# Sums of weight blocks by accumulating transfers, and signs moved into the forms: one core, retention and two dense layers

## The chip, the cores and the metric

The kernel runs on one core of one Trainium2 chip. The metric is device time in microseconds (us) of one execution; lower is better. The engines are TensorE (PE; its weight loads are listed as PEld), VectorE (DVE), ScalarE (ACT), GpSimd (POOL) and SyncE (SP), which only issues transfers here. Each engine works through its own instructions in order and waits on semaphores for the others.

## The reference

Three parts follow one another: retention (a recurrent state per head), a first dense layer with a hard-swish, and a second layer of eight experts whose results are weighted by a matrix P and summed.

```python
# retention: y[t] = scale * q[t] @ state;  state = gamma*state + k[t]^T v[t]
h = x @ w_in;  g = h * clip(h + 3, 0, 6) / 6;  x = g @ w_out     # 1536 x 512, 2048
logits = x @ w_gate
P = exp(logits - logits.max())                                   # 1536 x 8
# 8 times: P /= P.sum(1) + 1e-9;  P /= P.sum(0) + 1e-9;  P *= 1536 / 8
for e in range(8):
    h = maximum(x @ w1[e], 0)                                    # 512 -> 1024
    out += P[:, e:e+1] * (h @ w2[e])                             # 1024 -> 512
```

## The kernel before

All matmuls of the two layers take each float32 operand as a high part (rounded, by a ScalarE copy to the type fp32r) and a low part (what is left, by a VectorE subtraction), and sum three products: high x high, high x low, low x high. The helper `parts` makes the two parts.

The first layer goes through blocks of 512 tokens. `stage_a` makes h (12 matmuls), then ScalarE writes t (L353), VectorE multiplies it by h (L355), ScalarE writes its high part ghi (L358) and VectorE its low part glo (L360); `stage_b` multiplies by w_out two stages later. In the last block of the first layer (from step LASTB on) the loop also calls `next(forming)` four times a step: this prepares the second layer. In the same steps the gate's logits are made: `logits` multiplies on TensorE and copies to SBUF on ScalarE (tile l, L414), `logits_to_rows` transposes l on TensorE one step later (tile lt, L420).

The second layer works on two units of 768 tokens (unit u uses y2[u]). The weights of a unit go through 32 pairs of blocks (`pair(i)`, i from 0 to 63 over both units). The first expert matmul of a pair is a 2 x 2 block product done with seven products instead of eight (Winograd's variant of Strassen's method): the weights give seven forms (A11, A12, A22 and the sums S1 to S4 of blocks of 128 x 256), made by `w1_forms(i)` one pair ahead; the tokens give seven forms (B11, B21, B22 and the differences T1 to T4), made once per unit by `x_forms(u)` into tiles with one buffer each. `product` runs six matmuls of 384 columns for one product. `pair` combines the products in four PSUM banks: a copy to p, to u, to p again on ScalarE (L604), additions on VectorE (L603). A bank into which TensorE accumulates further has to be copied first: S3 x T3 goes into the bank that u was copied from. `relu_parts` splits the results (gh, gl); `outputs` multiplies them with w2 one iteration (two pairs) later, in chunks of three matmuls of 512 columns, spread between the products.

What sets the order: one Python program emits all instructions, and each engine takes its own in that order. Generators spread the small work: in the loop over pairs, after each product of a pair a `slot` passes, in which `outs` emits output chunks and `next(job)` is called twice (once in the first iteration), each call running `w1_forms` or `w2_parts` to its next `yield`. At the change of unit (pair 32), `forming` (the x forms of unit 1 and one set of weight forms) is started beside eight chunks of outputs that run alone. The loads: `load_pair(i, 0)` loads the two halves of w1 blocks for pair i, `load_pair(i, 1)` those of w2, all on SP, each into one of two buffers, two pairs ahead; SP waits until the buffer's old contents have been read.

## Time and profile before

| what | value |
|---|---|
| time, three runs | 1329.68, 1330.94, 1335.48 us; median 1330.94 us |
| span of the profiled execution (first to last instruction) | 1329.5 us; no separate time of this execution is given |
| TensorE busy | 1318.1 us, 99% of the span |
| VectorE busy | 897.7 us, 68% |
| ScalarE busy | 567.6 us, 43% |
| GpSimd busy | 26.7 us, 2% |
| DMA | 100.82 MB, mean 76 GB/s |

How to read it: an engine's busy time is the time in which it executed at least one instruction; an engine whose share is far below 100% can still be the one that others wait for at one place. The span runs from the first to the last instruction of one execution; the times are those of other executions without the profile.

### The profile page before, as it was taken

What the parts mean: (1) busy time and instruction counts of PE and PEld (TensorE: products, weight loads), DVE (VectorE), ACT (ScalarE), POOL (GpSimd) and SP (SyncE); (2) the same over time, 40 slices, a digit from 0 to 9 for tenths busy, and PEclk for the clock granted to TensorE, in tenths of its full rate; (3) what the DMA queues carried; (4) which work ended last, traced back from release to release, by engine and by line L of the source; (5) the groups of instructions that cost most, each with busy time, mean ns of one, the idle gap of its engine ahead of it and who ended that gap; (6) DMA issues with size and microseconds to landing.
All of it is one profiled execution on the core that took longest, in us unless ns stands there. A gap on an engine that the chain in (4) does not pass through costs nothing.

```text
span 1329.5 us, 17332 instructions
## 1 busy us (share of the span) xinstructions
PE 1318.1 (99%) x6776; PEld 1164.4 (88%) x6776; DVE 897.7 (68%) x1704; ACT 567.6 (43%) x1072; POOL 26.7 (2%) x30
## 2 busy tenths in 40 slices
PE   8999999999999999999999999999999999999998
PEld 7888888888888999999999998899999999999997
DVE  6877657338688666666666668766666666666663
ACT  5567445224534343434443344444343434443340
POOL 4300000000000000000000000000000000000000
PEclk9999999999999999999999999999999999999999
DMA  8633222002212122111221211312222111221201
GB/s 309 217 95 96 64 64 80 0 0 66 93 49 75 68 67 76 64 64 64 67 77 65 78 64 57 119 64 76 68 67 77 64 64 64 71 73 65 79 17 48
DMA packets 44990, 100.82 MB, mean 76 GB/s; under 512 B 3430, under 2 KB 3430, under 8 KB 44908
## 3 DMA queue, kind: packets, MB, share of 16 engines
q1 hardware_dynamic: 44908, 99.71, 22.2%
q8 instruction: 53, 0.87, 0.3%
q14 instruction: 29, 0.24, 0.1%
HBM read 96.55 MB, written 3.15 MB: 75 GB/s over the span
## 4 chain that ended last, share of the span: by engine, by line
PE 90%; DVE 3%; ACT 1%; DMA 0%; issue 0%; ACTq 0%
PE acc L660 38%; PE h L585 33%; PE acc L375 10%; PE h L348 9%; DMA raw<-in_we 0%; DVE gl L596 0%; DVE xl L501 0%; DVE w1lo L501 0%; DVE o L673 0%; DVE w2lo L501 0%; PE l L405 0%; DVE o L669 0%; DVE p L603 0%; ACT w2hi L500 0%; ACT xh L500 0%
## 5 line engine op out<-in xcount | busy, mean ns | idle before, releaser
L585 PE MATMUL h<-xh,w1hi 128*128 128x384 f32 x896 | 301.8, 337 | 0.9 <-ACT p L604 0.9
L660 PE MATMUL acc<-w2hi,gl 128*128 128x512 f32 x768 | 301.7, 393 | 0.0
L585 PE MATMUL h<-xh,w1lo 128*128 128x384 f32 x896 | 301.1, 336 | 0.0
L585 PE MATMUL h<-xl,w1hi 128*128 128x384 f32 x896 | 300.8, 336 | 0.2 <-DVE xl L501 0.2
L660 PE MATMUL acc<-w2hi,gh 128*128 128x512 f32 x768 | 299.6, 390 | 0.0
L660 PE MATMUL acc<-w2lo,gh 128*128 128x512 f32 x768 | 298.8, 389 | 0.0
L673 DVE SCALAR_TENSOR_TENSOR o<-acc,pm,o 128x512 f32<-128x512 f32 x174 | 130.7, 751 | 143.7 <-PE acc L660 143.7
L585 PEld LDWEIGHTS h<-xl,w1hi 128*128 128x128 f32 x896 | 168.2, 188 | 20.3 <-DVE xl L501 0.9
L585 PEld LDWEIGHTS h<-xh,w1hi 128*128 128x128 f32 x896 | 168.3, 188 | 19.8 <-ACT p L604 1.6
L660 PEld LDWEIGHTS acc<-w2hi,gl 128*128 128x128 f32 x768 | 144.1, 188 | 30.9
L585 PEld LDWEIGHTS h<-xh,w1lo 128*128 128x128 f32 x896 | 168.2, 188 | 0.0
L660 PEld LDWEIGHTS acc<-w2lo,gh 128*128 128x128 f32 x768 | 144.3, 188 | 13.0
L660 PEld LDWEIGHTS acc<-w2hi,gh 128*128 128x128 f32 x768 | 143.8, 187 | 13.0
L604 ACT ACTIVATE p<-h 128x384 f32<-128x384 f32 x128 | 62.9, 491 | 203.2 <-PE h L585 203.1
L501 DVE TENSOR_TENSOR w1lo<-raw,w1hi 128x512 fp32r<-128x512 f32 (+1 forms) x128 | 71.1, 555 | 77.4 <-ACT w1hi L500 77.3
L501 DVE TENSOR_TENSOR w1lo<-s,w1hi 128x512 fp32r<-128x512 f32 x128 | 87.9, 688 | 37.9 <-ACT w1hi L500 37.7
L604 ACT ACTIVATE u<-h 128x384 f32<-128x384 f32 x64 | 31.5, 492 | 173.5 <-PE h L585 173.5
L595 ACT ACTIVATE gh<-p 128x384 fp32r<-128x384 f32 x128 | 66.7, 521 | 57.5 <-DVE p L603 57.5
L501 DVE TENSOR_TENSOR w2lo<-raw,w2hi 128x512 fp32r<-128x512 f32 x128 | 87.2, 683 | 4.7 <-ACT w2hi L500 4.7
L595 ACT ACTIVATE gh<-u 128x384 fp32r<-128x384 f32 x64 | 33.6, 525 | 127.3 <-DVE u L603 127.3
L500 ACT ACTIVATE w1hi<-s 128x512 fp32r<-128x512 f32 x128 | 79.7, 624 | 3.3 <-DVE s L520 1.9
L348 PE MATMUL h<-xhi,wlo 128*128 128x512 f32 x192 | 74.9, 390 | 0.5 <-DVE wlo L136 0.5
(107 smaller groups left out, 1681.3 us busy)
## 6 DMA issues: line engine op xcount, KB each, us to landing
raw<-in_we SPq DMA_DIRECT2D x128, 512.0 KB, 3.4
raw<-in_wf SPq DMA_DIRECT2D x32, 512.0 KB, 3.7
qk<-in_qk SPq DMA_DIRECT2D x12, 512.0 KB, 6.9
kv<-in_kv SPq DMA_DIRECT2D x12, 512.0 KB, 6.0
out<-o SPq DMA_DIRECT2D x12, 256.0 KB, 2.0
tab<-in_tab SPq DMA_DIRECT2D x1, 40.5 KB
gk<-in_gk SPq DMA_DIRECT2D x1, 24.0 KB, 3.5
wg_raw<-in_wg SPq DMA_DIRECT2D x1, 16.0 KB, 7.7
```

The source lines that it names most:

```text
L348: nc.tensor.matmul(h, w[:, ks], x[:, k], start=(n == 0), stop=(n == 3 * KT - 1))
L375: nc.tensor.matmul(acc_b[i], l, r, start=(f == 0 and j == 0), stop=(f == nf - 1 and j == 2))
L500: nc.scalar.activation(out=hi, in_=t, func=AF.Copy)
L501: nc.vector.tensor_tensor(out=lo, in0=t, in1=f32(hi), op=ALU.subtract)
L585: nc.tensor.matmul(bank[:, 0:SB], l[:, w, ks], r[:, k], start=(start and n == 0), stop=(stop and n == 5), skip_group_check=True,)
L595: nc.scalar.activation(out=hi, in_=t, func=AF.Relu)
L604: copy = lambda out, a: nc.scalar.activation(out=out, in_=a, func=AF.Copy)
L660: nc.tensor.matmul(acc, l[:, cs], r[:, f % 2], start=(f == 0 and k == 0), stop=(f == 3 and k == 2))
L673: nc.vector.scalar_tensor_tensor(out=o[:, tt], in0=acc, scalar=sc, in1=o[:, tt], op0=ALU.mult, op1=ALU.add)
```

## The change

The four sums S1 to S4 of a pair's weight blocks are no longer formed by VectorE from the raw tile. `load_sums` builds them while loading: one plain transfer on SP writes block a21 four times (a broadcast read) into the tile s, then three transfers on POOL with the accumulate operation add further blocks from the weights in memory: a22 to the first three parts, a11 to the last three of four, as `block(1, 1, 3)` and `block(0, 0, 3)`, and a12 to the third. The sums are therefore all-plus sums, and the order of the forms changes to S1, S2, S4, S3. The raw tile holds only a11, a12 and a22 (two loads on SP). The signs that this takes away move to other places: `parts` can make the negative of a form (scale -1 in the ScalarE copy, another VectorE operation for the low part), used for B11 and B22; two copies in `pair` carry the scale -1; one addition becomes a subtraction. `x_forms` makes T1, T2, T4 and T3 in one buffer, xt, that is rewritten in place. `w1_forms` has three steps instead of seven, `x_forms` seven instead of nine, and `load_pair(i + 2, 0)` stands at the end of `w1_forms(i)`.

```diff
--- before.py
+++ after.py
@@ -482,23 +482,49 @@
 
 
 
-    A11, A12, A22, S1, S3, S2, S4 = range(7)
+    A11, A12, A22, S1, S2, S4, S3 = range(7)
     B11, T2, T1, T3, B21, B22, T4 = range(7)
-    xf, w1_t, w2_t, raw1, raw2, q_t = {}, {}, {}, {}, {}, {}
+    xf, w1_t, w2_t, raw1, raw2, q_t, sum_t = {}, {}, {}, {}, {}, {}, {}
 
     def load_pair(i, part):
         if i >= NIT:
             return
         f = 2 * (i % NPR)
-        t = pools["m2" if part else "m"].tile([P, 2, BLK], F32, tag=f"raw{part}", name=f"raw{part}", bufs=2)
-        nc.sync.dma_start(
-            out=t, in_=we_in[f:f + 2, :, part * BLK:(part + 1) * BLK].rearrange("t p c -> p t c")
-        )
-        (raw1, raw2)[part][i] = t
-
-    def parts(hi, lo, t):
-        nc.scalar.activation(out=hi, in_=t, func=AF.Copy)
-        nc.vector.tensor_tensor(out=lo, in0=t, in1=f32(hi), op=ALU.subtract)
+        if part == 0:
+            t = pools["m"].tile([P, 3, BLK // 2], F32, tag="raw0", name="raw0", bufs=2)
+            nc.sync.dma_start(out=t[:, 0:2], in_=we_in[f, :, 0:BLK].rearrange("p (k c) -> p k c", k=2))
+            nc.sync.dma_start(out=t[:, 2], in_=we_in[f + 1, :, BLK // 2:BLK])
+            raw1[i] = t
+            load_sums(i)
+            return
+        t = pools["m2"].tile([P, 2, BLK], F32, tag="raw1", name="raw1", bufs=2)
+        nc.sync.dma_start(out=t, in_=we_in[f:f + 2, :, BLK:2 * BLK].rearrange("t p c -> p t c"))
+        raw2[i] = t
+
+    def load_sums(i):
+
+        f = 2 * (i % NPR)
+        H2 = BLK // 2
+        t = pools["m"].tile([P, 4, H2], F32, tag="s", name="s", bufs=2)
+
+        def block(r, k, n):
+            a = we_in[f + r, :, k * H2:(k + 1) * H2].rearrange("p (o c) -> p o c", o=1)
+            return a.to_broadcast([P, n, H2]) if n > 1 else a
+
+        nc.sync.dma_start(out=t, in_=block(1, 0, 4))
+        nc.gpsimd.dma_start(out=t[:, 0:3], in_=block(1, 1, 3), accum_op=ALU.add)
+        nc.gpsimd.dma_start(out=t[:, 1:4], in_=block(0, 0, 3), accum_op=ALU.add)
+        nc.gpsimd.dma_start(out=t[:, 2:3], in_=block(0, 1, 1), accum_op=ALU.add)
+        sum_t[i] = t
+
+    def parts(hi, lo, t, sign=1):
+        nc.scalar.activation(out=hi, in_=t, func=AF.Copy, scale=float(sign))
+        if sign > 0:
+            nc.vector.tensor_tensor(out=lo, in0=t, in1=f32(hi), op=ALU.subtract)
+        else:
+            nc.vector.scalar_tensor_tensor(
+                out=lo, in0=t, scalar=-1.0, in1=f32(hi), op0=ALU.mult, op1=ALU.subtract
+            )
 
     def w1_forms(i):
 
@@ -506,23 +532,13 @@
         H2 = BLK // 2
         hi = pools["m"].tile([P, 7, H2], F32R, tag="w1hi", name="w1hi", bufs=2)
         lo = pools["m"].tile([P, 7, H2], F32R, tag="w1lo", name="w1lo", bufs=2)
-        a11, a12, a21, a22 = (r[:, f, k * H2:(k + 1) * H2] for f in range(2) for k in range(2))
-        t = pools["m"].tile([P, 4, H2], F32, tag="s", name="s", bufs=2)
-        parts(hi[:, A11:A12 + 1], lo[:, A11:A12 + 1], r[:, 0].rearrange("p (k c) -> p k c", k=2))
-        yield True
-        nc.vector.tensor_tensor(out=t[:, S1 - S1], in0=a21, in1=a22, op=ALU.add)
-        yield True
-        nc.vector.tensor_tensor(out=t[:, S3 - S1], in0=a11, in1=a21, op=ALU.subtract)
-        yield True
-        nc.vector.tensor_tensor(out=t[:, S2 - S1], in0=t[:, S1 - S1], in1=a11, op=ALU.subtract)
-        parts(hi[:, A22], lo[:, A22], a22)
-        yield True
-        nc.vector.tensor_tensor(out=t[:, S4 - S1], in0=a12, in1=t[:, S2 - S1], op=ALU.subtract)
-        load_pair(i + 2, 0)
+        t = sum_t.pop(i)
+        parts(hi[:, A11:A22 + 1], lo[:, A11:A22 + 1], r)
         yield True
         for n in range(2):
-            parts(hi[:, S1 + 2 * n:S3 + 1 + 2 * n], lo[:, S1 + 2 * n:S3 + 1 + 2 * n], t[:, 2 * n:2 * n + 2])
+            parts(hi[:, S1 + 2 * n:S1 + 2 * n + 2], lo[:, S1 + 2 * n:S1 + 2 * n + 2], t[:, 2 * n:2 * n + 2])
             yield True
+        load_pair(i + 2, 0)
         w1_t[i] = (hi, lo)
 
     def w2_parts(i):
@@ -542,37 +558,32 @@
         )
         xf.clear()
 
-        def form(n, t):
+        def form(n, t, sign=1):
             xf[n] = tuple(pools["xf"].tile([P, 2, SB], F32R, tag=f"x{n}{p}", name=f"x{p}") for p in "hl")
-            parts(*xf[n], t)
-
-        def tmp():
-            t = pools["m"].tile([P, 4, BLK // 2], F32, tag="s", name="s", bufs=2)
-            return t.rearrange("p a b -> p (a b)")[:, 0:2 * SB].rearrange("p (k c) -> p k c", k=2)
-
-        form(B11, b11)
+            parts(*xf[n], t, sign)
+
+        t = pools["m"].tile([P, 2, SB], F32, tag="xt", name="xt", bufs=1)
+
+        def into(a, b):
+            nc.vector.tensor_tensor(out=t, in0=a, in1=b, op=ALU.subtract)
+
+        form(B11, b11, -1)
         yield True
         form(B21, b21)
         yield True
-        t1 = tmp()
-        nc.vector.tensor_tensor(out=t1, in0=b12, in1=b11, op=ALU.subtract)
-        t2 = tmp()
-        nc.vector.tensor_tensor(out=t2, in0=b22, in1=t1, op=ALU.subtract)
+        into(b12, b11)
+        form(T1, t)
         yield True
-        form(T2, t2)
+        into(b22, t)
+        form(T2, t)
         yield True
-        form(T1, t1)
+        into(b21, t)
+        form(T4, t)
         yield True
-        t4 = tmp()
-        nc.vector.tensor_tensor(out=t4, in0=b21, in1=t2, op=ALU.subtract)
-        t3 = tmp()
-        nc.vector.tensor_tensor(out=t3, in0=b22, in1=b12, op=ALU.subtract)
+        into(b12, b22)
+        form(T3, t)
         yield True
-        form(T3, t3)
-        yield True
-        form(B22, b22)
-        yield True
-        form(T4, t4)
+        form(B22, b22, -1)
         yield True
 
     def product(i, bank, w, x, start, stop):
@@ -601,12 +612,12 @@
         tmp = lambda n: pools["m2"].tile([P, SB], F32, tag=n, name=n, bufs=2)
         bank = lambda n: ps_s.tile([P, BLK], F32, tag=n, name="h")
         add = lambda out, a, b: nc.vector.tensor_tensor(out=out, in0=a, in1=b, op=ALU.add)
-        copy = lambda out, a: nc.scalar.activation(out=out, in_=a, func=AF.Copy)
+        copy = lambda out, a, sign=1: nc.scalar.activation(out=out, in_=a, func=AF.Copy, scale=float(sign))
 
         bx = bank("s0")
         product(i, bx, A11, B11, True, True)
         p1 = tmp("p1")
-        copy(p1, bx[:, 0:SB])
+        copy(p1, bx[:, 0:SB], -1)
         yield
         by = bank("s1")
         product(i, by, A12, B21, True, True)
@@ -614,7 +625,7 @@
         add(p1, by[:, 0:SB], p1)
         product(i, bx, S2, T2, False, True)
         u2 = tmp("u2")
-        copy(u2, bx[:, 0:SB])
+        copy(u2, bx[:, 0:SB], -1)
         yield
         relu_parts(i, 0, 0, p1)
         bz = bank("r")
@@ -628,7 +639,7 @@
         product(i, bz, S4, B22, False, True)
         relu_parts(i, 1, 1, p5)
         yield
-        add(u2, bz[:, 0:SB], u2)
+        nc.vector.tensor_tensor(out=u2, in0=u2, in1=bz[:, 0:SB], op=ALU.subtract)
         product(i, bx, A22, T4, False, True)
         yield
         relu_parts(i, 0, 1, u2)
```

What this moves, on ScalarE, at three places. First the last block of the first layer, from the second stage that ScalarE handles beside the forms on (xh are the x forms' high parts, w1hi those of the weight forms, l the copy of the logits). Before:

```order
L353 ACTIVATE t<-h,three 128x512
L358 ACTIVATE ghi<-t 128x512
L500 ACTIVATE xh<-s 128x768 x2
L353 ACTIVATE t<-h,three 128x512
L358 ACTIVATE ghi<-t 128x512
L500 ACTIVATE xh<-s 128x768
L500 ACTIVATE xh<-x_726 128x768
L500 ACTIVATE xh<-s 128x768
L500 ACTIVATE w1hi<-raw_2480 128x512
L414 ACTIVATE l<-l 128x384
L353 ACTIVATE t<-h,three 128x512
L358 ACTIVATE ghi<-t 128x512
```

With the change (L521 is the copy in `parts`, L500 before):

```order
L353 ACTIVATE t<-h,three 128x512
L358 ACTIVATE ghi<-t 128x512
L521 ACTIVATE xh<-xt 128x768 x4
L353 ACTIVATE t<-h,three 128x512
L358 ACTIVATE ghi<-t 128x512
L521 ACTIVATE xh<-x_726 128x768
L521 ACTIVATE w1hi<-raw_2480 128x768
L521 ACTIVATE w1hi<-s 128x512 x2
L414 ACTIVATE l<-l 128x384
L353 ACTIVATE t<-h,three 128x512
L358 ACTIVATE ghi<-t 128x512
```

The four difference forms stand together ahead of the next t, and three copies of weight forms, two of them from s, stand between ghi and the second l; before, there was one between them.

Second, the change of unit (pair 32), from the first x forms of unit 1 on. Before:

```order
L500 ACTIVATE xh<-x_727 128x768 x2
L500 ACTIVATE xh<-s 128x768
L604 ACTIVATE p_7224<-h 128x384
L500 ACTIVATE xh<-s 128x768
L604 ACTIVATE u_7255<-h 128x384
L500 ACTIVATE xh<-s 128x768
L595 ACTIVATE gh<-p_7224 128x384
L604 ACTIVATE p_7275<-h 128x384
```

With the change (lines from `pair` on are 11 higher: L615 is the copy that was L604):

```order
L521 ACTIVATE xh<-x_727 128x768 x2
L521 ACTIVATE xh<-xt 128x768 x2
L615 ACTIVATE p_7203<-h 128x384
L521 ACTIVATE xh<-xt 128x768 x2
L615 ACTIVATE u_7236<-h 128x384
L521 ACTIVATE xh<-x_727 128x768
L606 ACTIVATE gh<-p_7203 128x384
L615 ACTIVATE p_7256<-h 128x384
```

The copy to u stands behind the high parts of all four difference forms; before, it stood behind those of two difference forms.

Third, the steady loop, one pair from its first copy to p on. Before:

```order
L604 ACTIVATE p_6767<-h 128x384
L500 ACTIVATE w1hi<-raw_6540 128x512
L500 ACTIVATE w1hi<-raw_6540 128x256
L604 ACTIVATE u_6803<-h 128x384
L500 ACTIVATE w1hi<-s 128x512
L595 ACTIVATE gh<-p_6767 128x384
L604 ACTIVATE p_6829<-h 128x384
L500 ACTIVATE w1hi<-s 128x512
L500 ACTIVATE w2hi<-raw_6582 128x512 x2
```

With the change:

```order
L615 ACTIVATE p_6610<-h 128x384
L521 ACTIVATE w1hi<-raw_6365 128x768
L521 ACTIVATE w1hi<-s 128x512 x2
L521 ACTIVATE w2hi<-raw_6396 128x512
L615 ACTIVATE u_6656<-h 128x384
L521 ACTIVATE w2hi<-raw_6396 128x512
L606 ACTIVATE gh<-p_6610 128x384
L615 ACTIVATE p_6681<-h 128x384
L606 ACTIVATE gh<-p_6681 128x384
```

All copies of the next pair's weight forms, and the first of w2, now stand ahead of the copy to u; before, two stood there.

## Rows read from the trace of the kernel before

**Rows 1.** The page, parts 1 and 2: busy time, and clock in 40 slices.

```profile
PE 1318.1 (99%) x6776; PEld 1164.4 (88%) x6776; DVE 897.7 (68%) x1704; ACT 567.6 (43%) x1072; POOL 26.7 (2%) x30
...
PEclk9999999999999999999999999999999999999999
```

**Rows 2.** Windows: stretch, length, busy us of each engine, clock, DMA share, GB/s.

```profile
325.00:345.00 20.00, 19.64 (x111) 17.72 (x110) 16.08 (x33) 12.17 (x26) 0.00 (x0) 1.00 0.38 127
375.00:800.00 425.00, 424.33 (x2134) 383.38 (x2133) 297.83 (x605) 169.78 (x352) 0.00 (x0) 1.00 0.20 67
800.00:830.00 30.00, 29.84 (x147) 26.15 (x146) 24.66 (x40) 14.66 (x27) 0.00 (x0) 1.00 0.17 62
830.00:860.00 30.00, 29.48 (x151) 26.67 (x150) 24.20 (x47) 14.37 (x30) 0.00 (x0) 1.00 0.38 132
860.00:1300.00 440.00, 440.00 (x2211) 398.28 (x2210) 295.53 (x564) 178.02 (x369) 0.00 (x0) 1.00 0.19 64
```

**Rows 3.** Timeline, ScalarE, two pairs: start, duration, instruction, idle before.

```profile
610.10 0.49 ACT L604 ACTIVATE p<-h 128x384 f32<-128x384 f32 x1 [2.66 <-PE h L585]
...
614.25 0.49 ACT L604 ACTIVATE u<-h 128x384 f32<-128x384 f32 x1 [2.83 <-PE h L585]
...
625.63 0.49 ACT L604 ACTIVATE p<-h 128x384 f32<-128x384 f32 x1 [2.66 <-PE h L585]
```

**Rows 4.** Groups by line and shape: busy us, mean ns.

```profile
L501 DVE TENSOR_TENSOR w1lo<-s,w1hi 128x512 fp32r<-128x512 f32 x128 | 87.9, 688 | 37.9 <-ACT w1hi L500 37.7
...
L500 ACT ACTIVATE w1hi<-s 128x512 fp32r<-128x512 f32 x128 | 79.7, 624 | 3.3 <-DVE s L520 1.9 <-DVE s L515 1.4
...
L513 DVE TENSOR_TENSOR s<-raw 128x256 f32<-128x256 f32 x64 | 26.8, 418 | 0.0
...
L159 DVE TENSOR_SCALAR w<-raw 128x512 uint32<-128x512 uint32 x32 | 14.5, 454 | 1.1 <-DMA raw<-in_wf 1.1
...
L501 DVE TENSOR_TENSOR xl<-s,xh 128x768 fp32r<-128x768 f32 x8 | 7.6, 956 | 2.3 <-ACT xh L500 2.3
...
L500 ACT ACTIVATE xh<-s 128x768 fp32r<-128x768 f32 x8 | 6.6, 837 | 8.3 <-DVE s L560 8.1 <-DVE s L569 0.3
```

**Rows 5.** The page, part 6: DMA issues, KB each, us to landing.

```profile
raw<-in_we SPq DMA_DIRECT2D x128, 512.0 KB, 3.4
...
qk<-in_qk SPq DMA_DIRECT2D x12, 512.0 KB, 6.9
...
out<-o SPq DMA_DIRECT2D x12, 256.0 KB, 2.0
```

**Rows 6.** Timeline, VectorE, last block of the first layer.

```profile
299.27 0.95 DVE L558 TENSOR_TENSOR s<-x 128x768 f32<-128x768 f32 x1
300.25 0.96 DVE L560 TENSOR_TENSOR s<-x,s 128x768 f32<-128x768 f32 x1
```

**Rows 7.** Timeline, ScalarE, the same stretch.

```profile
302.73 0.67 ACT L353 ACTIVATE t<-h,three 128x512 f32<-128x512 f32 x1
306.73 0.63 ACT L358 ACTIVATE ghi<-t 128x512 fp32r<-128x512 f32 x1 [3.33 <-DVE t L355]
...
310.00 0.47 ACT L414 ACTIVATE l<-l 128x384 f32<-128x384 f32 x1
```

**Rows 8.** The chain that ended last, the same stretch: start, us, what.

```profile
311.50 0.33 PE lt L420 x3
```

**Rows 9.** Timeline, VectorE, at the change of unit.

```profile
814.31 0.95 DVE L558 TENSOR_TENSOR s<-x 128x768 f32<-128x768 f32 x1
```

**Rows 10.** Timeline, ScalarE, at the change of unit.

```profile
817.47 0.49 ACT L604 ACTIVATE p<-h 128x384 f32<-128x384 f32 x1 [0.34 <-PE h L585]
...
820.94 0.49 ACT L604 ACTIVATE u<-h 128x384 f32<-128x384 f32 x1 [2.24 <-PE h L585]
```

**Rows 11.** Timeline, TensorE, the product S3 x T3 at the change of unit.

```profile
823.10 0.33 PE L585 MATMUL h<-xh,w1hi 128*128 128x384 f32 x1
823.60 0.45 PE L585 MATMUL h<-xl,w1hi 128*128 128x384 f32 x1 [0.16 <-DVE xl L501]
```

## The prediction

> **What bounds the kernel now.** Read the page first: TensorE is busy 1318.1 us of a span of 1329.5 us, and the granted clock is full in all forty slices [rows 1]. VectorE has 68% and ScalarE 43%. So the question is only where TensorE ever waits. The table by stage answers it for the second layer, which begins near 323 us: between 375 and 800 us TensorE idles 0.7 us of 425, between 860 and 1300 us not at all; 0.36 us are lost at the start of the layer and 0.7 us around the change of unit (800 to 860 us) [rows 2]. Work that is taken from VectorE or ScalarE in the steady loop can therefore return nothing. The loop's period is one pair of blocks: the copy of the first product begins at 610.10 us and one pair later at 625.63 us, so 15.53 us per pair [rows 3].
>
> **The change in the steady loop.** Removed from VectorE: four adds or subtracts of 128x256 per pair, 0.42 us each [rows 4], 1.7 us in all of a pair's 15.53; the two separate splits of the raw tile become one of 128x768. This is worth 0 us, since TensorE does not wait there [rows 2]. The other sign of a form and of an accumulation changes an instruction's scale or operation, not its size: 0 us.
>
> Moved: the splits of the next pair now stand together. On ScalarE the copy of the second result u used to follow one pass over the raw tile; now it follows a 128x768 copy (0.84 us, as the x form of that size), two of 128x512 (0.62 us each) and one w2 copy, taken at the same 0.62 us [rows 4]. From the end of the copy of p at 610.59 us that makes 613.3 us; TensorE does not release u before 614.25 us [rows 3]. So 0 us, with 0.95 us of cover. If the sums landed late, ScalarE would stand at its first copy from s, and u, p and the banks behind them would wait.
>
> Added: per pair one plain transfer of 512 KB on SP (instead of a part of the raw load) and three accumulating ones on POOL, 384, 384 and 128 KB. Each waits for the one before, and POOL takes them in order, so a pair costs POOL two waits for 384 KB and about one for 128 KB. With X and Y for the two sizes, the loop holds as long as 2X + Y stays under 15.53 us. No accumulating transfer is in the trace. A plain load of 512 KB lands in 3.4 us, a store of 256 KB in 2.0 us [rows 5]: 1.4 us per 256 KB and 0.6 us fixed. I count an accumulation as twice its bytes, because it reads the source and the old value: X = 0.6 + 3 x 1.4 = 4.8 us, Y = 2.0 us, 2X + Y = 11.6 us. The lower end counts the bytes once: 2.7 and 1.3, 6.7 us. The upper end takes the loads of the first stage, 6.9 us for 512 KB, and twice the bytes: 10.35 and 3.45, 24.2 us. I take 11.6 us, as DMA in this stage is busy only 0.19 to 0.20 at 64 to 67 GB/s [rows 2]; the change multiplies the bytes by 2304/1024, which with the extra reads of 896 KB makes about 0.6. It hides under TensorE's 15.53 us, with 3.9 us of cover: 0 us. The whole chain with its plain transfer takes 15.0 us, and with two buffers it has about two pairs, 31 us.
>
> The Trainium skill bears on this price. Its page "Collectives: The Full Stack" (section "The bandwidth ceiling: the fold count and why AG ≠ RS ≠ AR") says that an add inside a transfer costs two source reads, not cycles; its page "DMA: Bandwidth & Descriptors" (section "Anatomy of one DMA — SWDGE (gpsimd) path") gives 2.0 us plus bytes/436e3. By both, as an estimate, X would be 3.8 and Y 2.6, 2X + Y 10.2 us, and the sum the same.
>
> **The x forms, made twice, are where it costs.** Before, two temporaries of the tag s let VectorE run its subtractions back to back (299.27 and 300.25 us [rows 6]). Now one buffer xt is rewritten in place: subtract on VectorE, high part on ScalarE, low part on VectorE, and only then the next subtraction. A step takes 0.96 + 0.84 + 0.96 us [rows 4], 2.76 us, and there are four in a row.
>
> First place, the last block of the first layer. The chain starts at 299.27 us; its fourth high part ends at 299.27 + 3 x 2.76 + 0.98 + 0.84 = 309.4 us, and the order puts the activation t behind it, which ran at 302.73 us before [rows 7]. VectorE then does the fourth low part until 310.3 us, the reduction and t x h; ScalarE's second step ghi, 306.73 us before, starts at 311.2 us. Behind it come B22, the raw copy (768) and two copies from s, and only then l, the logits' copy: 311.2 + 0.54 + 0.74 + 0.75 + 1.05 = 314.25 us, ended 314.7 us, against a start of 310.00 us before. TensorE wants l for its transposes at 311.50 us [rows 8] and is in order, so the whole stream moves by 3.3 us. Nothing regains it: TensorE has no idle time behind. Bounds: 0 if l were not needed so soon, 5 if the steps run 10 to 15% slower.
>
> Second place, the change of unit. VectorE starts the first subtraction at 814.31 us [rows 9]; with 2.76 us per step and one accumulator update (0.66 us) between, the fourth high part ends at about 825.0 us. The copy of u, at 820.94 us before [rows 10], now stands behind it, ends near 825.5 us, and S3 x T3 needs its bank and the low part of T3, ready at 826.1 us. TensorE wanted that low part at 823.60 us [rows 11]. That is 2.5 us less about 0.3 us of the stalls that were there: +2.2 us, bounds 0 to 4.
>
> At the start of the second layer the load is less bunched but shares its DMA with the new transfers: 0 us, bounds -0.4 to +1.
>
> **Sum.** 3.3 + 2.2 = +5.5 us. On the profiled span of 1329.5 us that is 1335.0 us; the median of the three runs is 1.4 us above this span (1330.94), so I forecast 1336.4 us, +0.4%. About 0.5%, 6.65 us, is what a measurement of this kernel can tell from no change; so the forecast is "no change that can be told", near its edge.
>
> **Rivals.**
> A, slower by much: the accumulations are not hidden. If 2X + Y exceeds 15.53 us, POOL becomes the bound and every pair from the third on pays the excess, 62 times: X above 6.4 us decides it (Y at 0.4 X). At X = 7 the excess is 1.4 us and the time about 1423 us; at the upper end it is 8.6 us, 535 us more, about 1870 us. For it: 6.9 us for a plain 512 KB under load [rows 5]. Against it: 0.2 DMA share and 3.4 us in this very stage [rows 2, 5]. A mechanism of its own could bring it on: POOL kept from writing its descriptors while VectorE holds a common port. If each of the three waited for one of VectorE's longest instructions (0.96 us), 2X + Y would be 14.5 us, still hidden but with 1.0 us of cover. The Trainium skill's page "SBUF — State Buffer" ("The DVE blocks DMA trap (SWDGE)") states such a lock, for VectorE's faster two-port mode. The one-input operation of 128x512 takes 0.45 us, the two-input split w1lo<-s 0.69 us [rows 4], and the loop's splits are of the second kind.
>
> B, the x forms cost nothing: their stalls are covered in a way that I do not see, and the time is 1330 to 1332 us. For it: the page shows ScalarE idle more than half of the time [rows 1]. Against it: all engines work in order, and the places are fixed by the order.
>
> C, faster by over 0.5%: 6.65 us would have to come back, but the stages of the second layer hold 1.7 us of TensorE idle time altogether [rows 2]. Only a shorter spacing of matmuls could do it; nothing in the change touches that.
>
> **Chances.** Forecast (hidden transfers, two single stalls, 1332 to 1342 us) 0.64, of it 0.20 above 1337.6 us, since costs that I have not seen would add; B 0.08; A 0.25; C 0.03. So faster 0.03, same 0.44 + 0.08 = 0.52, slower 0.20 + 0.25 = 0.45. The range starts at 1330 us (C and half of B below it) and has to reach into A: up to 1400 us, an excess of 1.0 us per pair (X near 6.9 us), about half of A's weight; some 2 in 10 stay outside. The likeliest case's own range is 1332 to 1342 us.
>
> **What the profile after would show.** VectorE's busy time falls by some 110 us and TensorE's idle time does not fall. TensorE waits about 3 us for ScalarE's l before the second set of transposes near 311 us, and about 2 us near 823 us for u or the low part of T3. The accumulations on POOL land in 4 to 6 us, and no copy from s waits for DMA in the loop. The forecast is wrong if the period of a pair is above 15.53 us (A), if the two waits are missing (B), or if a third kind of wait appears, most likely in the first pairs, where a pair lasts only some 7 us and s, w1 and w2 loads come together.

## The result and the profile after

The changed kernel took 1347.31 us (median of 4 runs, 1346.28 to 1351.34); the kernel before, timed beside it, 1333.14 us (4 runs, 1329.68 to 1335.48). The ratio is 1.0114 [1.0094, 1.0134]: slower by 1.1%, some 14 us. That lies inside the range of 1330 to 1400 us, but the forecast of "no change that can be told" was missed: the median is 10.9 us above 1336.4 us. Six more runs of it (run 9) give 1.0099 [1.0076, 1.0122].

The page of the kernel after, parts 1 and 6 (KB each, us to landing), against [rows 1] and [rows 5]:

```profile
PE 1326.5 (99%) x6776; PEld 1170.4 (87%) x6776; DVE 812.7 (60%) x1384; ACT 565.4 (42%) x1008; POOL 248.1 (18%) x222
...
s<-in_we POOLq DMA_DIRECT2D x128, 384.0 KB, 5.0
s<-in_we SPq DMA_DIRECT2D x64, 512.0 KB, 5.4
...
s<-in_we POOLq DMA_DIRECT2D x64, 128.0 KB, 4.8
```

VectorE was relieved as intended, and TensorE, which bounds the kernel, is busy for 8.4 us longer with the same 6776 matmuls; 5.5 us of that lie ahead of the last block, which no edit touches (last section). An accumulation of 384 KB landed in 5.0 us (4.8 foreseen), the one of 128 KB in 4.8 us (2.0 foreseen).

The table by stage (busy us of each engine, clock, DMA share, GB/s), to be read beside [rows 2]:

```profile
375.00:800.00 425.00, 425.00 (x2142) 384.62 (x2142) 263.22 (x479) 171.85 (x332) 95.56 (x83) 1.00 0.70 154
...
830.00:860.00 30.00, 27.43 (x137) 24.05 (x136) 23.47 (x36) 16.38 (x30) 2.57 (x2) 1.00 0.62 160
860.00:880.00 20.00, 18.40 (x93) 16.39 (x93) 10.10 (x17) 7.12 (x14) 5.69 (x5) 1.00 0.71 152
880.00:1300.00 420.00, 420.00 (x2110) 380.38 (x2109) 249.07 (x409) 170.43 (x328) 92.29 (x80) 1.00 0.69 150
```

In the two long stretches TensorE never idles: in the loop the transfers are hidden. POOL's timeline there (start, duration, instruction, what ended the idle time before) shows one set of three in a pair, 15.43 us from one first transfer to the next:

```profile
599.81 1.28 POOL L515 DMA_DIRECT2D s<-in_we  x1 [5.22 <-DVE p L614]
604.83 1.28 POOL L516 DMA_DIRECT2D s<-in_we  x1 [3.74 <-DMA s<-in_we]
610.25 0.90 POOL L517 DMA_DIRECT2D s<-in_we  x1 [4.14 <-DMA s<-in_we]
615.24 1.28 POOL L515 DMA_DIRECT2D s<-in_we  x1 [4.10 <-DVE p L614]
```

What is lost is lost in single places. TensorE's waits (us in total, times, longest):

```profile
PE h L596 <- ACT u L615: 3.7, 2, 2.1
PE lt L420 <- ACT l L414: 3.5, 1, 3.5
PE h L596 <- ACT p L615: 1.9, 2, 1.6
```

The three that are not the wait for l, on TensorE's timeline (pair 1, the change of unit, and 30 us behind it):

```profile
344.44 0.45 PE L596 MATMUL h<-xh,w1hi 128*128 128x384 f32 x1 [1.63 <-ACT p L615]
...
837.16 0.44 PE L596 MATMUL h<-xh,w1hi 128*128 128x384 f32 x1 [2.07 <-ACT u L615]
...
866.95 0.44 PE L596 MATMUL h<-xh,w1hi 128*128 128x384 f32 x1 [1.60 <-ACT u L615]
```

Where the time went is read by landmarks on ScalarE that both programs have: the 42nd activation t of the first layer (the start of its last block, here), and the copies to u of pairs 0, 5, 31, 35 and 63. Lengths in us, worked out from ScalarE's timelines:

| profiled run | start | last block | first pairs (u0 to u5) | u5 to u31 | unit change (u31 to u35) | u35 to u63 |
|---|---|---|---|---|---|---|
| before | 279.21 | 46.71 | 69.46 | 405.27 | 63.60 | 434.93 |
| after | 283.45 | 53.12 | 71.13 | 404.70 | 68.40 | 433.89 |
| after, once more (run 9) | 278.26 | 51.75 | 72.33 | 404.70 | 69.09 | 433.95 |

Between before and after: +6.4 us in the last block, +1.7 in the first pairs, +4.8 at the unit change, -1.6 in the two stretches between, and +4.2 at the start, which no edit touches. Run 9 without the slow start: +5.0, +2.9, +5.5, -1.5 and -1.0, 10.9 us in all.

The -1.6 us are no gain in the loop. With the change ScalarE makes the copy to u later behind the copy to p in two of these pairs (4.44 us in pair 31 and 5.19 in pair 35, against 4.15 and 4.14 before), without TensorE waiting for it, so these landmarks move by themselves; and 1.1 us come back between pairs 5 and 6, ahead of the steady loop. The first copy to p of a pair does not: in each of these pairs ScalarE stands idle until TensorE releases it. By it:

| profiled run | last block (to p0) | first pairs (p0 to p6) | p6 to p31 | unit change (p31 to p35) | p36 to p63 |
|---|---|---|---|---|---|
| before | 44.63 | 84.33 | 388.33 | 63.61 | 419.40 |
| after | 51.04 | 85.14 | 388.33 | 67.65 | 419.40 |
| after, once more (run 9) | 49.67 | 86.36 | 388.33 | 68.38 | 419.40 |

So the steady loop is the same to the hundredth, and the loss is +6.4, +0.8 and +4.0 us in the profile after, +5.0, +2.0 and +4.8 us in run 9. The runs below give the u landmarks, and p where it matters.

**Last block.** ScalarE's timeline after, beside [rows 7]:

```profile
304.48 0.85 ACT L521 ACTIVATE xh<-xt 128x768 fp32r<-128x768 f32 x1 [1.63 <-DVE xt L568]
307.34 0.85 ACT L521 ACTIVATE xh<-xt 128x768 fp32r<-128x768 f32 x1 [2.02 <-DVE xt L568]
...
313.07 0.85 ACT L521 ACTIVATE xh<-xt 128x768 fp32r<-128x768 f32 x1 [2.02 <-DVE xt L568]
...
317.71 1.13 ACT L521 ACTIVATE w1hi<-s 128x512 fp32r<-128x512 f32 x2
318.75 0.47 ACT L414 ACTIVATE l<-l 128x384 f32<-128x384 f32 x1
```

The four high parts stand 2.86 us apart (2.76 foreseen), ScalarE idles about 2 us before each, and l comes at 318.75 us. With the later start of the block (4.24 us) taken off, that is 314.5 us, where 314.25 was foreseen. The windows over that place show more than a wait:

```profile
315.00:320.00 5.00, 1.45 (x8) 0.99 (x7) 4.26 (x7) 4.09 (x7) 0.00 (x0) 0.81 0.01 2
320.00:322.00 2.00, 2.00 (x6) 1.61 (x6) 1.30 (x3) 1.24 (x2) 0.00 (x0) 0.50 0.70 221
322.00:324.00 2.00, 2.00 (x6) 1.52 (x6) 1.96 (x4) 1.16 (x3) 0.00 (x0) 0.50 0.82 202
324.00:326.00 2.00, 2.00 (x9) 1.58 (x8) 0.53 (x3) 0.69 (x1) 0.01 (x1) 0.76 0.74 216
326.00:328.00 2.00, 2.00 (x10) 1.66 (x9) 1.30 (x2) 0.63 (x1) 1.26 (x1) 1.00 0.86 253
```

After the idle 3.5 us the granted clock is 0.50, the 1.2 GHz level, for about five microseconds: 6 matmuls per 2 us where 10 fit later. So a wait of 3.5 us costs 6.4 us.

**First pairs.** The wait of 1.63 us stands behind a w2 load that came late on ScalarE, not behind a sum:

```profile
340.18 0.63 ACT L521 ACTIVATE w2hi<-raw 128x512 fp32r<-128x512 f32 x1 [2.08 <-DMA raw<-in_we]
```

In run 9 it is the sums: there TensorE waits 0.93 us for p and 1.78 us for l, each behind a copy from s.

**Unit change.** SP issues the plain transfers of two sums at 843.35 and 848.84 us, because the sums before them were read only 5 us apart. POOL's timeline then:

```profile
847.91 1.28 POOL L515 DMA_DIRECT2D s<-in_we  x1 [18.84 <-DVE w1lo L523]
855.84 1.29 POOL L516 DMA_DIRECT2D s<-in_we  x1 [6.65 <-DMA s<-in_we]
861.77 0.91 POOL L517 DMA_DIRECT2D s<-in_we  x1 [4.64 <-DMA s<-in_we]
862.36 1.62 POOL L515 DMA_DIRECT2D s<-in_we  x1
868.11 1.28 POOL L516 DMA_DIRECT2D s<-in_we  x1 [4.12 <-DMA s<-in_we]
876.75 0.90 POOL L517 DMA_DIRECT2D s<-in_we  x1 [7.37 <-DMA s<-in_we]
```

and ScalarE's copies from these sums:

```profile
861.55 0.63 ACT L521 ACTIVATE w1hi<-s 128x512 fp32r<-128x512 f32 x1 [2.13 <-issue]
865.37 0.63 ACT L521 ACTIVATE w1hi<-s 128x512 fp32r<-128x512 f32 x1 [3.18 <-DMA s<-in_we]
...
879.75 0.63 ACT L521 ACTIVATE w1hi<-s 128x512 fp32r<-128x512 f32 x1 [2.39 <-DMA s<-in_we]
```

The first sum was whole 22 us after its plain issue, the second 31 us (to 879.75), for its three transfers had to stand behind the first one's on POOL. ScalarE, in order, holds u and p back until the sum is there. The first of these sums is TensorE's wait of 1.60 us at 866.95 us; at the second TensorE does not wait.

### The profile page after: what moved, and what is told of

Same layout as the page of the kernel before. It is cut to its first block, busy times and chain, and to the rows that moved or that the text cites. A ratio compares the mean times of both kernels' runs of the same rounds, so it can differ in the third digit from the quotient of the medians.

```text
span 1345.0 us, 17793 instructions
## 1 busy us (share of the span) xinstructions
PE 1326.5 (99%) x6776; PEld 1170.4 (87%) x6776; DVE 812.7 (60%) x1384; ACT 565.4 (42%) x1008; POOL 248.1 (18%) x222
## 4 chain that ended last, share of the span: by engine, by line
PE 88%; DVE 3%; ACT 1%; DMA 1%; issue 1%; POOL 0%; DVEq 0%; ACTq 0%; POOLq 0%
PE acc L671 38%; PE h L596 33%; PE acc L375 9%; PE h L348 9%; DMA s<-in_we 1%; DVE xl L523 1%; ACT xh L521 1%; DVE xt L568 1%; DMA raw<-in_we 1%; DVE w2lo L523 0%; DVE o L684 0%; DVE t L355 0%; DVE w1lo L523 0%; DVE x L392 0%; ACT w1hi L521 0%
## 5 line engine op out<-in xcount | busy, mean ns | idle before, releaser
L515 POOL DMA_DIRECT2D s<-in_we x64 | 87.5, 1366 | 425.5 <-DMA s<-in_we 312.5
L615 ACT ACTIVATE p<-h 128x384 f32<-128x384 f32 x128 | 62.8, 491 | 205.3 <-PE h L596 204.8
L516 POOL DMA_DIRECT2D s<-in_we x64 | 81.8, 1278 | 267.3 <-DMA s<-in_we 267.3
L614 DVE TENSOR_TENSOR p<-h,p 128x384 f32<-128x384 f32 x128 | 70.8, 553 | 95.0 <-PE h L596 95.0
L523 DVE TENSOR_TENSOR w1lo<-raw,w1hi 128x768 fp32r<-128x768 f32 x64 | 61.3, 957 | 90.2 <-ACT w1hi L521 90.2
L517 POOL DMA_DIRECT2D s<-in_we x64 | 57.6, 900 | 313.1 <-DMA s<-in_we 309.3
L523 DVE TENSOR_TENSOR w1lo<-s,w1hi 128x512 fp32r<-128x512 f32 x128 | 83.0, 685 | 11.7 <-ACT w1hi L521 11.7
```

The source lines that it names most:

```text
L515: nc.gpsimd.dma_start(out=t[:, 0:3], in_=block(1, 1, 3), accum_op=ALU.add)
L516: nc.gpsimd.dma_start(out=t[:, 1:4], in_=block(0, 0, 3), accum_op=ALU.add)
L517: nc.gpsimd.dma_start(out=t[:, 2:3], in_=block(0, 1, 1), accum_op=ALU.add)
L523: nc.vector.tensor_tensor(out=lo, in0=t, in1=f32(hi), op=ALU.subtract)
L614: add = lambda out, a, b: nc.vector.tensor_tensor(out=out, in0=a, in1=b, op=ALU.add)
L615: copy = lambda out, a, sign=1: nc.scalar.activation(out=out, in_=a, func=AF.Copy, scale=float(sign))
```

## The experiments

The theory: the loss has two causes, the chained x forms (a wait, and half clock behind it) and sums that come late where pairs are close together. Rivals: contention by 2304 KB a pair everywhere, one cause alone, or a loss no longer than the wait.

**Run 1, e1_xforms_as_before.** The changed kernel with the differences formed two at a time again.

```diff
-        def into(a, b):
+        def into(t, a, b):
...
-        into(b12, b11)
-        form(T1, t)
+        into(b11, b12, b11)
+        into(t, b22, b11)
         yield True
-        into(b22, t)
         form(T2, t)
         yield True
-        into(b21, t)
-        form(T4, t)
+        form(T1, b11)
...
```

> The changed kernel with the x forms made in the order of before: two differences ahead, then their parts (the second buffer is the x tile itself, written in place); the loads, the accumulating transfers and the signs stay. Theory (the in-place chain of the x forms is most of the loss: 3.5 us of waiting for the logits' copy, some 2.7 us of matmuls at half clock behind it, some 2 us at the change of unit): 8 us less than the changed kernel, so about 1339 us where the changed kernel has 1347; no wait for l near 315 us, granted clock 1.00 in that stretch. Rival (the accumulating transfers are the loss): within 2 us of the changed kernel.

Measured: 1343.84 us, ratio 1.0082 [1.0055, 1.0109]. The last block is 46.72 us, as before the change, and clock and wait of that place are gone. But the first pairs grew to 73.73 and the unit change to 70.99 us. ScalarE's timeline there:

```profile
855.47 0.63 ACT L521 ACTIVATE w1hi<-s 128x512 fp32r<-128x512 f32 x1 [6.40 <-issue]
858.83 0.63 ACT L521 ACTIVATE w1hi<-s 128x512 fp32r<-128x512 f32 x1 [2.73 <-DMA s<-in_we]
```

and TensorE's clock in the windows behind it:

```profile
860.00:862.00 2.00, 1.59 (x5) 1.59 (x6) 2.00 (x5) 1.59 (x4) 0.31 (x1) 0.50 0.81 167
862.00:864.00 2.00, 2.00 (x7) 1.71 (x6) 1.45 (x3) 0.71 (x2) 0.96 (x1) 0.50 0.76 199
```

The stalls of the x forms had given the sums time. Without them the wait for u behind the late sum grows from 1.6 to 5.4 us, with half clock behind it too, and in the first pairs TensorE waits 2.6 us for l. The two causes hide each other: undoing one returned 3.5 us by the medians, and by the profiles, from the last block on, only 0.2 us against after and 0.8 us against run 9.

**Run 2, e2_no_accumulation.** The three accumulating transfers left out.

```diff
         nc.sync.dma_start(out=t, in_=block(1, 0, 4))
-        nc.gpsimd.dma_start(out=t[:, 0:3], in_=block(1, 1, 3), accum_op=ALU.add)
-        nc.gpsimd.dma_start(out=t[:, 1:4], in_=block(0, 0, 3), accum_op=ALU.add)
-        nc.gpsimd.dma_start(out=t[:, 2:3], in_=block(0, 1, 1), accum_op=ALU.add)
```

> The changed kernel without the three accumulating transfers; it leaves out the additions to the sums, everything else runs. Theory (the x forms are most): only the waits of the first pairs of the second layer (some 2 us) and one after the change of unit (1.6 us) go, so 3 to 4 us less than the changed kernel, with the wait for l, the half clock and the wait at the change of unit as they are. Rival (the transfers are the loss): back to within 3 us of before.

Measured: 1340.33 us, ratio 1.0062 [1.0043, 1.0082]. First pairs 69.63 us (before: 69.46), unit change 66.90 (63.60), last block 53.29 (46.71). What stays is the x forms: 6.6 us in the last block and 3.3 us at the unit change, with TensorE's waits of 3.6 us for l and 2.1 us for u. The wait for u is as long as in the profile after, but here half clock follows it. Run 2:

```profile
833.00:835.00 2.00, 2.00 (x7) 1.91 (x7) 2.00 (x4) 0.83 (x2) 0.00 (x0) 0.50 0.37 133
```

and after, as far behind its own wait:

```profile
840.00:842.00 2.00, 1.75 (x9) 1.29 (x8) 2.00 (x4) 0.83 (x3) 0.00 (x0) 1.00 0.38 135
```

In runs 7 and 9 the same wait of 2.1 us brings 0.50 as well.

**Run 3, e3_both_undone.** Both edits above together.

```diff
-        nc.gpsimd.dma_start(out=t[:, 0:3], in_=block(1, 1, 3), accum_op=ALU.add)
...
-        into(b12, b11)
-        form(T1, t)
+        into(b11, b12, b11)
+        into(t, b22, b11)
...
```

> Both: x forms in the order of before, and no accumulating transfers (the additions to the sums are left out). Theory: the two parts are all there is, so within 2 us of before, although VectorE has some 110 us less to do; the relief of VectorE returns nothing. Rival (a further cost lies in the moved signs or in the splits that stand together in the loop): 3 us or more above before.

Measured: 1330.26 us, ratio 0.9982 [0.9964, 0.9999]; last block 46.70, first pairs 69.62, unit change 62.71 us. By p the first pairs take 83.54 us (84.33 before), the unit change 62.72 us (63.61) and the loops 388.33 and 419.40 us. The new signs and the new grouping of the splits cost nothing that shows; no third cause is left. From the last block on run 3 is 1.7 us shorter than before, in the stretches in which TensorE had idled before; that is all the relief of VectorE can have returned.

**Run 4, e4_late_logits_copy, and run 5, e5_short_logits_copy.** The kernel before with nothing but a later l: its second copy repeated 10 times, then 5 times.

```diff
-        nc.scalar.activation(out=l, in_=t[:, 0:SB], func=AF.Copy)
+        for _ in range(10 if n == 1 else 1):
+            nc.scalar.activation(out=l, in_=t[:, 0:SB], func=AF.Copy)
```

> The kernel before with one thing added: the second copy of the logits in the last block of the first layer is made ten times over (nine more of 0.49 us each, the same values), so that l comes late there and nowhere else. ScalarE issues such copies about 0.38 us apart, so l is 3.4 us later and TensorE waits some 2.5 to 3.4 us for it. Theory (a wait of this length also costs the clock behind it): some 5 to 6 us more than before, with a granted clock near 0.5 for 5 to 6 us after the wait. Rival (a wait costs only its length): 2.5 to 3.4 us more, clock 1.00.

> The kernel before with the second logits copy repeated 5 times instead of 10 (same output). Ten copies took 5.18 us and made TensorE wait 3.7 us, so 4 more copies of 0.52 us less the same slack of about 1.0 us give a wait of about 1.1 us. Theory (only the long pause brings the half clock behind it): the last-block segment grows by that wait alone, 46.7 to about 47.8 us, and the granted clock stays 1.00 from 310 to 330 us. Rival (the loss is in proportion to the wait, 6.7 for 3.7 us): about 48.7 us, with a stretch of lower clock behind the wait.

Measured: with ten copies 1338.04 us, ratio 1.0035 [1.0017, 1.0053], and the last block +6.7 us for a wait of 3.7 us; with five (one run, 1330.99 us) a wait of 1.1 us and the last block 48.02 us, +1.3. Windows with ten copies:

```profile
310.00:318.00 8.00, 4.27 (x13) 3.20 (x12) 2.95 (x7) 5.58 (x12) 0.00 (x0) 0.72 0.00 0
318.00:324.00 6.00, 6.00 (x23) 4.81 (x22) 3.00 (x8) 2.82 (x6) 0.00 (x0) 0.81 0.27 90
```

and with five:

```profile
310.00:318.00 8.00, 7.14 (x33) 5.99 (x34) 5.19 (x12) 5.02 (x10) 0.00 (x0) 1.00 0.19 61
318.00:324.00 6.00, 6.00 (x31) 5.26 (x30) 5.90 (x13) 2.22 (x5) 0.00 (x0) 1.00 0.28 99
```

The long wait lowers the clock, the short one does not, and the loss is not in proportion. A late l alone makes the last block's whole loss.

**Run 6, e6_one_more_accumulation.** One accumulating transfer of 384 KB twice.

```diff
         nc.gpsimd.dma_start(out=t[:, 1:4], in_=block(0, 0, 3), accum_op=ALU.add)
+        nc.gpsimd.dma_start(out=t[:, 1:4], in_=block(0, 0, 3), accum_op=ALU.add)
         nc.gpsimd.dma_start(out=t[:, 2:3], in_=block(0, 1, 1), accum_op=ALU.add)
```

> The changed kernel with the transfer that adds the first block a second time in three of the four sums (its sums are changed by that; the work of every engine but the queue is not). Theory (POOL's queue is full in the loop: the three transfers of a pair are issued 5.0, 5.4 and 5.0 us apart, 2X + Y = 11.6 us is its least by the prediction, and 15.53 us a pair is the limit): a fourth of 5.0 us makes about 16.6 us a pair, so the loop goes from 15.53 to about 16.6 us a pair, ScalarE waits for the sums in every pair, and the time is about 1347 + 60 x 1.07 = 1410 us. Rival (the transfers overlap, or the queue has room): the period stays 15.53 us and the time within 5 us of the changed kernel.

Measured: 1634.34 us (one run). The loop takes 530.98 / 26 = 20.4 us a pair, where the theory said 16.6 and its rival 15.53. POOL's timeline:

```profile
603.15 0.90 POOL L518 DMA_DIRECT2D s<-in_we  x1 [3.91 <-DMA s<-in_we]
603.74 1.61 POOL L515 DMA_DIRECT2D s<-in_we  x1
609.11 1.28 POOL L516 DMA_DIRECT2D s<-in_we  x1 [3.76 <-DMA s<-in_we]
619.09 1.28 POOL L517 DMA_DIRECT2D s<-in_we  x1 [8.70 <-DMA s<-in_we]
625.00 0.90 POOL L518 DMA_DIRECT2D s<-in_we  x1 [4.64 <-DMA s<-in_we]
```

POOL never waits for anything but its own transfers: it is the bound, as rival A had it. The size was missed because one of the transfers now lies beside the pair's loads on SP (512 KB for s at 607.56 us, 512 KB of w2 at 609.89 us), and it took 10.0 us where the others took 5.4 to 5.9; over the loop it took 6.3 to 10.0 us, 8.8 in the middle. In the changed kernel it is the small transfer that stands beside them, 4.8 us there and 3.0 us here. The clock falls too, to 0.91 from 600 to 700 us, since TensorE waits for u in nearly every pair (57 waits, 1.2 to 6.6 us, 194.5 us in all), but that lies under POOL's bound and adds nothing to it. The rows show one thing more: POOL issues the next sum's first transfer 0.59 us behind the small one (603.15, 603.74 us), so it does not wait for the small one to land.

**Run 7, e7_later_splits, and run 8, e8_xforms_and_later_splits.** In each pair the w2 splits go first, and the splits of the sums behind them, one a slot; run 8 has the x forms of run 1 as well.

```diff
-                    jobs.append([w1_forms(i + 1)] if ahead else [])
-                    jobs[-1].append(w2_parts(i))
+                    jobs.append([w2_parts(i)])
+                    jobs[-1] += [w1_forms(i + 1)] if ahead else []
...
-                        for _ in range(1 if not it or (alone and slot < 6) else 2):
+                        for _ in range(2 if alone and 6 <= slot <= 8 else 1):
```

> The changed kernel with the jobs of a pair in another order: the splits of the second-layer weights first, those of the sums behind them and one step per slot instead of two, so each split of a sum is asked for some 4 to 6 us later in its pair. Nothing else is changed. Theory (sums that come late are what is left beside the x forms): the waits of ScalarE for s go, the first pairs take about 69.6 us (71.13) and the unit change about 66.9 us (68.40), as without accumulations; the last block stays 53; about 1344 us. Rival (contention of the transfers, not their lateness): the segments stay at 71 and 68, about 1347 us.

> The changed kernel with its x forms in the order of the kernel before (differences formed two at a time, in place in the input tile), and the splits of the sums asked for later in each pair as in the run above. Theory (the two costs are the x forms and the late sums, and nothing else): last block 46.7, first pairs about 69.6, unit change about 62.7 us, as with both undone; about 1331 us, that is the kernel before or up to 2 us less. Rival (the sums are late by more than the splits were moved): first pairs and unit change stay 2 to 7 us longer, 1335 to 1343 us.

Measured: run 7 took 1339.60 us, ratio 1.0048 [1.0030, 1.0066], with first pairs 70.48 and unit change 66.71 us, the latter as with no accumulation at all. Run 8 took 1330.02 us, ratio 0.9981 [0.9964, 0.9998]: last block 46.72, first pairs 71.14, unit change 62.72 us. All transfers run, and what ScalarE waits for sums in the whole of run 8 (12.0 us in 8 waits in run 9) is

```profile
ACT w1hi L521 <- DMA s<-in_we: 1.3, 2, 1.1
```

Between run 1 and run 8 only the order and pace of the splits differ, and that is worth 13.8 us by the medians, 11.2 us by the profiles from the last block on. The sums were late, not expensive. In the first pairs the theory missed: they were to take 69.6 us, and 0.9 us (run 7) and 1.5 us (run 8) stay, where ScalarE waits 1.3 and 2.0 us for the first w2 load and TensorE 0.8 and 1.5 us for p behind it. Without the accumulating transfers (run 3) that load is not waited for, so there the rival, contention of the transfers, fits. Run 8 is the fastest kernel with the whole computation, 2.4 us below before by the medians, which is under the 0.5% that can be told safely; by the profiles, from the last block on, the two are equal within 0.2 us. It is also no faster than run 3, which leaves the transfers out.

**Run 9, e9_changed_again.** The changed kernel, unaltered, for its start.

> The changed kernel once more, unaltered, for more times of it. The profiled execution spent 283.45 us up to the last block where other kernels with the same code there took 277.5 to 283.5, so part of its 14 to 15 us may be an unlucky start and not the change. If so (first reading), the median falls to about 1342 to 1345 us, the ratio to 1.007 to 1.010, and the segments behind the start are again 53 (last block), 71 (first pairs), 68 (unit change). If the four times were typical (second reading), the median is 1347 us again and the start near 283 us.

Measured: 1347.08 us (6 runs, 1341.64 to 1349.57). Neither reading holds alone: two runs are near 1342 us, one of them the profiled one with a start of 278.26 us, and four from 1346.94 us up. The two kinds of start occur in other kernels too (run 7's profile 282.80 us, run 8's 278.59 us). Whether the unprofiled runs near 1347 us had the slow one is not shown; if so, why the changed kernel met it so often is open.

**Run 10, e10_half_pace.** The chain kept, but two pieces of forming work a step in place of four.

```diff
             if s >= LASTB:
-                for _ in range(2):
+                for _ in range(1):
                     next(forming, None)
```

> The changed kernel with one piece of forming work in place of two at each of the two calls of a step in the last block; the pieces and their order are kept, the rest goes to the steps behind. Theory (TensorE waits because the logits copy stands behind four chained x forms on ScalarE, not because the forms are longer in all): with two chained forms fewer ahead of it the copy comes about 2 x 2.86 = 5.7 us earlier, the wait of 3.5 us and the half clock behind it go, and the last block takes about 46.7 to 47.5 us (53.1); the unit change keeps its 68.4 us; about 6 us less than the changed kernel. Rival (the chain only moves the stall): the forms left over end late, ScalarE and VectorE finish the first pair's weights after TensorE is ready, and the last block and first pairs together stay at about 124 us.

Measured: 1353.86 us, ratio 1.0150 [1.0123, 1.0178]. Of the theory the first half came true: the last block is 46.70 us, with no wait for l and full clock. But the first pairs took 87.64 us, so together 134.3 against 124.3 us, 10 us more than the rival had. The unit change kept its time by p (68.29 us, 67.65 in after). The forms ended later, so the loads for s, behind them on SP, were issued at 324.5 and 329.0 us (320.2 and 324.4 in after), and the w2 loads right behind, from 329.4 us on (333.4), while the second layer began 7 us sooner (p0 at 327.46 us, 334.49 in after). ScalarE's timeline of the first pair and TensorE's windows:

```profile
338.59 0.63 ACT L521 ACTIVATE w2hi<-raw 128x512 fp32r<-128x512 f32 x1 [7.52 <-DMA raw<-in_we]
```

```profile
335.00:340.00 5.00, 0.79 (x5) 0.46 (x3) 0.75 (x2) 1.41 (x3) 0.00 (x0) 0.87 0.83 206
340.00:350.00 10.00, 5.05 (x15) 4.55 (x16) 4.62 (x8) 3.17 (x7) 2.96 (x3) 0.50 0.56 135
```

So moving the x forms back did not help here; making them quicker (run 1 with run 7's splits, which is run 8) did.

## Why the prediction was right and wrong

**The loop at 0 us: right.** The period stayed at 15.53 us (388.33 / 25 and 419.40 / 27, as before), though DMA was busy 0.70 of the time (0.6 foreseen). VectorE gave up 85.0 us, not 110: three of its four adds of 0.42 us had started 0.33 us apart (611.76, 612.09, 612.43 us before), so their durations overlap. As foreseen, that returned nothing in the loop.

**2X + Y = 11.6 us: right in X (4.8 foreseen, 5.0 measured), wrong in Y (2.0 foreseen, 4.8 measured) and in that POOL waits for Y.** The conclusion, hidden under 15.53 us, held all the same. In the loop POOL's three issues follow one another after 5.0, 5.4 and 5.0 us, the last of these a wait for the next plain transfer, issued at 609.48 us and 5.4 us to land (the row names VectorE's p); run 6 shows the next sum issued 0.59 us behind the small transfer. Of the Trainium skill's fit ("DMA: Bandwidth & Descriptors", section "Anatomy of one DMA — SWDGE (gpsimd) path"), which gave the estimates of 3.8 and 2.6 us, both measured values lie above. Run 6 showed that the cover of 3.9 us could not have taken another transfer of 5 us, nor been sized by adding one: the fourth made the pair 4.9 us longer.

**The wait for l, +3.3 us: right as a wait (3.5 us), wrong as a cost (5.0 to 6.4 us).** The step that failed is "so the whole stream moves by 3.3 us". TensorE came out of the wait at half clock. In all profiled runs, from 70 us on, the waits that began at full clock and lasted 2.0 us or less left it at 1.00, and those of 2.66 us or more brought 0.50 behind them; run 6 alone has 16 of the one and 32 of the other. In between both occur: 2.1 us for u left 1.00 in the profile after and brought 0.50 in runs 2, 7 and 9, and 2.6 us for l left 1.00 in run 1. The Trainium skill's page "TensorE: Matmul & The Clock Gate", section "HAM oscillation — how this bites in real kernels", says that work after a long enough gap starts throttled; the long waits of these runs agree.

**The unit change, +2.2 us: right for its wait (2.1 us for u), wrong for its sum.** In the profile after it cost 4.0 us by p: the 2.1 us foreseen, at full clock, and 1.6 us behind a late sum. In runs 2, 7 and 9 half clock followed the same wait; there the x forms cost 3.3 us (run 2), and a late sum 1.4 us more (run 9).

**"At the start of the second layer [...] 0 us, bounds -0.4 to +1": wrong, with the chain's "15.0 us, and with two buffers it has about two pairs, 31 us".** This is the second step that failed. A chain takes some 21 us even in the loop (plain issue at 593.94 us, the last add issued at 610.25 us and 4.8 us to land), and 22 us at the unit change, where the copy wanted the sum after 19 us; two chains that are asked for 5 us apart share POOL, so the second takes 31 us; and after two quick pairs the copies ask for it sooner. Against run 2, which has no accumulations, the first pairs cost 1.6 us (after) to 2.8 us (run 9) by p: a late w2 load in the one, late sums in the other. At the unit change late sums cost about 1.5 us. The prediction named a wait in the first pairs as what would make it wrong, but gave it no price, and did not see it at the unit change.

**The range held by luck.** The forecast's own case was 1332 to 1342 us, and 1347.31 us lies 5.3 us above it. It lies inside 1330 to 1400 us only because the range was stretched into rival A, whose mechanism, POOL as the bound, did not happen.

**Rivals.** A did not happen; run 6 shows that it was one transfer away, and how steep it is. Whether any of the 5.0 us of an accumulation is the lock between VectorE and POOL that A names, no run tests. B falls (run 2). C falls: nothing came back beyond 2 us (run 3).

By run 9's profile and p the loss is 10.9 us: 5.0 us in the last block and 3.3 us (by run 2) at the unit change for the x forms, 2.8 and 1.5 us in the first pairs and at the unit change for late sums, less 0.8 us by which run 2 is shorter than before in the first pairs, and 0.95 at the start. The medians differ by some 3 to 4 us more, as far as the profiles tell because of the start; where the unprofiled runs spent it is not shown.

## What to carry to other kernels

Price a wait of the engine that bounds the kernel by its length and by the clock behind it, and merge or shorten the long ones first: here waits of 2.0 us and less paid their length alone, one of 2.1 us either its length or 1.4 to 1.8 us more, and those for l of 3.5 us and more about 1.4 to 1.8 times their length. A chain of transfers that replaces arithmetic must be whole before the closest pair of readers asks for it, not before the average one; look where its buffers are read close together, and move the readers back before blaming the transfers. When two edits each cause a stall, undo both, since either alone can hide the other. Before a gain or a loss is read between two landmarks, choose landmarks that the bounding engine releases, since another engine's can move by itself.

## What was not expected of the hardware

In the slow starts the count of matmuls and the record of the clock do not fit together. From 8 to 18 us TensorE is always busy and the granted clock reads 1.00 in both rows, yet it gets through 68 matmuls in the profile of after,

```profile
8.00:18.00 10.00, 10.00 (x68) 7.33 (x66) 4.30 (x7) 3.52 (x7) 5.68 (x6) 1.00 0.73 284
```

and 122 in run 9 with the same code:

```profile
8.00:18.00 10.00, 10.00 (x122) 8.34 (x122) 7.01 (x11) 5.55 (x11) 7.14 (x7) 1.00 1.01 394
```

This is where the 5 us of the start lie; its cause stays open. An accumulation of 384 KB took 5.4 us by itself but 6.3 to 10.0 us, 8.8 in the middle, beside two loads of 512 KB (run 6). And one and the same wait of TensorE, 2.1 us for u, left the clock at full in one run of a kernel and halved it in another run of that same kernel (after and run 9).
